# Retention and a gated feed-forward layer in one kernel: weight sums on another engine and at another place, and a cast and a decay factor that change places

## The chip, the cores and the metric

The kernel runs on one core of a Trainium2 chip. A core has five engines with a queue of instructions each: TensorE (PE, with its weight loads shown apart as PEld), VectorE (DVE), ScalarE (ACT), GpSimd (POOL) and SyncE (SP), which here only issues transfers. The engines meet by semaphores alone. The metric is the device time of one execution in microseconds (us); lower is better.

## The reference, cut to what matters

```python
# q, k, v: (8 batches, 8 heads, 576 positions, 64), float32
scores = q @ k^T / sqrt(64)
gamma  = 1 - 2 ** (-5 - head)
ret    = (scores * gamma ** (i - j) for j <= i, else 0) @ v
x      = ret, heads side by side, as (4608 tokens, 512)
out    = (sigmoid(x @ w_gate) * (x @ w_val)) @ w_out      # 512 -> 1536 -> 512
```

The decay gamma ** (i - j) splits into gamma ** i on the row of q and gamma ** (-j) on the row of k. In a sum over j, the second factor may stand on k or on v: the score with j is always multiplied by row j of v, and so is row j of k in the running state k^T v.

## The kernel before, in words

**Retention.** The first 768 columns of x are made by a start-up part that works on pairs of tiles. The rest is cut into 30 steps, s = 0 to 29, each of 128 positions of one batch (STEPS, L101). Step s loads its k, q and v from HBM (`load`, L161), each 256 KB as 128x512 float32, and casts them to bf16 (`cast_qk`, L397; `cast_v`, L410): q is multiplied by a table of gamma ** i (`qtab`), k by a table of gamma ** (-j) (`ktab`), and v is copied. From s = 11 on (SCALED_V, L408), ScalarE casts k plainly and GpSimd multiplies v by `ktab`. A transfer on SP's queue (`cross`, L418) then turns q and k into T_s; for s = 0, 1 and 7 TensorE does that (`turn_step`, L596). The order of one step is written in `casts_to` (L870): issue the loads of a later step, cast k, cast q, turn, cast v. TensorE makes scores, the products k^T v and the values out of this (`slot`, L709, for one step; `slot_of_two`, L725, for two). Copies to x and to the running state follow piece by piece (`after`, L828). `next_slot` (L881) calls the slot of step s and then the casts of step s+3.

**Feed-forward.** x is worked off in blocks of columns (BLOCKS, L344): 512 columns made by the start-up part, then the two small blocks of 256 at columns 512 and 768, called the first and the second 256 block here, then seven of 512. In the small ones `h_units` (L899) makes gate and value for two rows of 128 at a time, fc = 0, 2, 4, 6, 8, 10: the gate product goes to a bank of PSUM and ScalarE takes its sigmoid (L911), the value product goes to the next bank and VectorE multiplies both (L913). These banks come from a ring of three, so the value product of fc + 2 takes the bank that the sigmoid of fc has read. `op_units` (L1246) multiplies by w_out.

The blocks of 512 use a multiplication scheme with seven products of quarter matrices in place of eight (`quarter_units`, L988; `quarters`, L1101). It needs sums of quarters of the weights: sums into tables of their own (`w_sums`, L336, and `wo_sums`, L310, i = 0, 1, 3) and one in place per group (i = 2), which overwrites a quarter of w_gate, w_val or w_out. An in-place sum may come only after the small blocks, which need the raw weights, have read that quarter.

**Order.** All of it is written out by hand. A loop (L1535 to L1580) goes through the blocks; for each unit i of TensorE's work it adds one entry of `weight_sums` at odd i in the two small blocks (L1554), the in-place sums that PLACES (L1085) puts there, and one piece of the retention's work. Each engine does its instructions in the order in which they were written.

Of the kernel before, what the change touches and what calls it, by code (L numbers as in the profile page):

```python
# [16 lines left out]
def kernel(  # L17
# [19 lines left out]
    nc = tc.nc  # L37
# [272 lines left out]
    def wo_sums(i, part, parts, eng=nc.vector):  # L310

        fp = slice(part * (NFC // 2) // parts, (part + 1) * (NFC // 2) // parts)
        b11, b12, b21, b22 = (wo_sb[:, r::2, c:c + DM // 2][:, fp] for r in range(2) for c in (0, DM // 2))
        t1, t2, t4 = (wt_sb[:, j, fp] for j in range(3))
        to, a, b = ((t1, b12, b11), (t2, b22, t1), (b12, b22, b12), (t4, b21, t2))[i]
        eng.tensor_tensor(out=to, in0=a, in1=b, op=ALU.subtract)
# [19 lines left out]
    def w_sums(kind, i, u, eng):  # L336

        a11, a12, a21, a22 = w_quarters(kind, u)
        s1, s2, s4 = (wt3_sb[kind][j][:, u] for j in range(3))
        to, a, b, op = ((s1, a21, a22, ALU.add), (s2, s1, a11, ALU.subtract), (a21, a11, a21, ALU.subtract),  # L340
                        (s4, a12, s2, ALU.subtract))[i]
        eng.tensor_tensor(out=to, in0=a, in1=b, op=op)
# [50 lines left out]
    def by_halves(x):  # L393

        return x.rearrange("p (y m) d -> p y m d", y=2)

    def cast_qk(s, i, eng):  # L397
        c = STEPS[s][1]
        if i == 1:
            natural_qk[s] = nat_pool.tile([P, 2, M, P], BF16, tag="qk", name=f"qk_{s}")  # L400
        to = natural_qk[s][:, i].rearrange("p m (y d) -> p y m d", y=2)
        if i == 1 and s >= SCALED_V:
            nc.scalar.copy(out=to, in_=by_halves(loaded[s][0]))
            return
        tab = (qtab, ktab)[i][:, c, :].rearrange("p (y m) -> p y m", y=2).unsqueeze(3).to_broadcast([P, 2, M, D])
        eng.tensor_tensor(out=to, in0=by_halves(loaded[s][1 - i]), in1=tab, op=ALU.mult)  # L406

    SCALED_V = 11  # L408

    def cast_v(s, eng):  # L410
        natural["v", s] = nat_pool.tile([P, H, D], BF16, tag="v", name=f"v_{s}", bufs=6)
        if s >= SCALED_V:
            tab = ktab[:, STEPS[s][1], :].unsqueeze(2).to_broadcast([P, H, D])
            nc.gpsimd.tensor_tensor(out=natural["v", s], in0=loaded[s][2], in1=tab, op=ALU.mult)  # L414
        else:
            eng(out=natural["v", s], in_=loaded[s][2])
# [453 lines left out]
    def casts_to(s):  # L870
        while done["cast"] <= min(NS - 1, s):
            x = done["cast"]
            loads_to(x + (AHEAD[x] if x < len(AHEAD) else 2))
            cast_qk(x, 1, nc.gpsimd)
            cast_qk(x, 0, nc.vector if x < 2 else nc.gpsimd)
            if x not in TURNED:
                cross(x)
            cast_v(x, on_dve if x == 0 else on_pool)
            done["cast"] += 1
# [108 lines left out]
    def quarter_units(gvs, t0):  # L988
# [82 lines left out]
        def value(fc):  # L1071
# [3 lines left out]
            for kc in range(NKC):  # L1075
# [6 lines left out]
        return quarter, value  # L1082

    EARLY = ((10, "g01"), (13, "g05"), (13, "g02"))
    PLACES = (((1, 0), "w", 0), ((1, 3), "g", 1), ((2, 0), "g", 0), ((2, 6), "o", 2), ((2, 7), "o", 0),  # L1085
              ((2, 10), "g", 2), ((2, 17), "w", 1), ((2, 43), "o", 1))
    TURN_AT = -1
    CASTS_AT = (2, 12)
    SECOND = 7
# [431 lines left out]
    casts_to(1)  # L1521

    weight_sums = [lambda kind=kind, u=u, i=i: w_sums(kind, i, u, nc.vector) for kind, u in (("w", 1), ("g", 2)) for i in (0, 1, 3)]
    weight_sums += [lambda u=u, i=i: wo_sums(i, u, 3) for u in range(3) for i in (0, 1, 3)]

    SPARE = {}
    for at, kind, u in PLACES:
        SPARE.setdefault(at, []).append((lambda u=u: wo_sums(2, u, 3)) if kind == "o" else (lambda kind=kind, u=u: w_sums(kind, 2, u, nc.vector)))
# [83 lines left out]
```

## Time and profile before

| | us |
|---|---|
| median of the runs | 309.91 |
| lowest, highest run | 309.65, 313.43 |
| the profiled execution | 310.84 |
| its span, first to last instruction | 308.9 |

| engine | busy us in the span | share |
|---|---|---|
| PE | 301.0 | 97% |
| DVE | 235.7 | 76% |
| ACT | 199.3 | 65% |
| POOL | 193.0 | 62% |

The profiled execution lies 0.93 us above the median. Its span leaves 1.94 us before the first and after the last instruction. The profile's page gives these sums; an answer of its timeline gives each instruction with its start, its duration and, in brackets, how long its engine stood idle before it and who ended that. Where a date is given below ("at 61.07") it is microseconds from the start of the span. The first 256 block starts at 51.12, the second at 70.32, the first block of 512 at 89.50. TensorE's granted clock is 1.00 in all stages.

### The profile page before, as it was taken

How to read it: one execution, taken by the hardware profiler on the slowest of the kernel's cores; microseconds unless marked ns; L12 is line 12 of the kernel's file. 1: busy time of each engine (PE TensorE's matmuls, PEld its weight loads, DVE VectorE, ACT ScalarE, POOL GpSimd, SP SyncE). 2: the span in 40 equal slices, each digit the busy share in tenths (PEclk: the TensorE clock that was granted, in tenths of full speed). 3: DMA queues.
4: the chain of work that ended last, by engine and by line, in shares of the span. 5: the costliest groups of instructions: out<-in, count | busy, mean ns of one | idle time of the engine just before them, and what ended most of it. 6: DMA issues, size and time to landing. Idle time of an engine off the chain costs nothing.

```text
span 308.9 us, 10407 instructions
## 1 busy us (share of the span) xinstructions
PE 301.0 (97%) x4286; PEld 235.8 (76%) x4286; DVE 235.7 (76%) x469; ACT 199.3 (65%) x408; POOL 193.0 (62%) x221
## 2 busy tenths in 40 slices
PE   8999999999999999999899999999999999999995
PEld 7674456868768778877788788878887888788874
DVE  6957957977889797698669976986699659844963
ACT  6755454535469648964797389737973797359720
POOL 5785653644576897579557965796578607810780
PEclk9999999999999999999999999999999999999999
DMA  7999999989999997990779589946881182004013
GB/s 222 341 371 387 347 272 211 219 168 151 246 191 221 270 218 171 227 219 2 141 175 254 120 139 203 252 95 138 191 211 47 36 280 96 4 2 137 3 34 102
DMA packets 145423, 54.97 MB, mean 178 GB/s; under 512 B 124384, under 2 KB 137696, under 8 KB 145376
## 3 DMA queue, kind: packets, MB, share of 16 engines
q1 hardware_dynamic: 144352, 53.66, 71.1%
q8 instruction: 33, 0.54, 0.7%
q10 hardware_dynamic: 1024, 0.66, 0.7%
q14 instruction: 14, 0.11, 0.1%
HBM read 37.75 MB, written 9.44 MB: 153 GB/s over the span
## 4 chain that ended last, share of the span: by engine, by line
PE 89%; DVE 4%; ACT 3%; POOL 1%; issue 1%; DVEq 0%
PE gatea L1027 11%; PE qa L1134 10%; PE qe L1134 9%; PE wa L1027 8%; PE h L1076 7%; PE gatee L1027 6%; PE we L1027 4%; PE op L1250 3%; PE op L1475 3%; PE gateg L1027 3%; PE hg L1326 3%; PE hv L1326 3%; PE h_g L908 3%; PE h_v L908 2%; PE val L689 2%; PE wg L1027 2%
## 5 line engine op out<-in xcount | busy, mean ns | idle before, releaser
L1027 PEld LDWEIGHTS <-wg_sb 128*128 128x128 bf16 x336 | 32.9, 98 | 5.6
L1050 POOL TENSOR_TENSOR gv<-gv,wu 128x512 bf16<-128x512 bf16 x14 | 16.3, 1166 | 31.7 <-DVE wu L1062 31.7
L1134 PEld LDWEIGHTS <-gsum 128*128 128x128 bf16 x312 | 29.9, 98 | 3.7
L406 POOL TENSOR_TENSOR qk<-q,qtab 128x512 bf16<-128x512 f32 x28 | 30.7, 1098 | 1.9 <-PE wa L1027 1.3
L963 POOL TENSOR_TENSOR gsum<-gv 128x512 bf16<-128x512 bf16 (+1 forms) x28 | 27.6, 987 | 5.3 <-DVE gv L1050 5.2
L1027 PEld LDWEIGHTS <-wgt_sb 128*128 128x128 bf16 x252 | 24.6, 98 | 3.4
L1076 PE MATMUL h<-xT,wv_sb 128*128 128x512 bf16 x112 | 26.5, 379 | 0.0
L1027 PE MATMUL gatea<-xsum,wg_sb 128*128 128x256 bf16 x168 | 25.2, 273 | 0.0
L1134 PEld LDWEIGHTS <-gv 128*128 128x128 bf16 x228 | 21.8, 98 | 4.0
L1027 PEld LDWEIGHTS <-wv_sb 128*128 128x128 bf16 x224 | 21.9, 98 | 3.6 <-issue 1.1
L406 POOL TENSOR_TENSOR qk<-k,ktab 128x512 bf16<-128x512 f32 x11 | 12.2, 1113 | 19.9 <-DMA k<-in_k_dram 14.9
L675 DVE TENSOR_TENSOR pt<-row,tri 128x512 bf16<-128x512 f32 (+1 forms) x36 | 20.0, 596 | 4.0 <-PE row L666 2.9
L1050 POOL TENSOR_TENSOR gv<-gv,ws 128x512 bf16<-128x512 bf16 x14 | 17.1, 1221 | 7.3 <-DVE ws L1065 7.3
L414 POOL TENSOR_TENSOR v<-v,ktab 128x512 bf16<-128x512 f32 x19 | 21.5, 1130 | 0.1
L1065 DVE TENSOR_TENSOR gs<-gatea,gs 128x512 f32<-128x512 f32 x21 | 14.4, 685 | 9.0 <-PE gatea L1027 8.4
L1062 DVE TENSOR_TENSOR gu<-gatee,gu 128x512 f32<-128x512 f32 x21 | 14.4, 687 | 8.4 <-ACT gateg L1054 3.5
L1079 DVE TENSOR_TENSOR gv<-gv,h 128x512 bf16<-128x512 bf16 x28 | 18.4, 678 | 2.4 <-PE h L1076 2.4
L1048 ACT ACTIVATE gv<-gs 128x512 bf16<-128x512 f32 x21 | 13.6, 647 | 9.6 <-DVE gs L1065 9.6
L1076 PEld LDWEIGHTS <-wv_sb 128*128 128x128 bf16 x112 | 11.0, 98 | 10.4
L1027 PEld LDWEIGHTS <-wvt 128*128 128x128 bf16 x168 | 16.4, 98 | 2.5 <-issue 0.6
L986 POOL TENSOR_TENSOR xsum<-xT 128x512 bf16<-128x512 bf16 x6 | 7.0, 1158 | 18.0 <-ACT xT L762 13.1
L762 ACT CAST xT<-val 128x512 bf16<-128x512 f32 x22 | 12.5, 592 | 8.1 <-PE val L705 8.1
(192 smaller groups left out, 859.5 us busy)
## 6 DMA issues: line engine op xcount, KB each, us to landing
k<-in_k_dram SPq DMA_DIRECT2D x26, 256.0 KB, 3.9
q<-in_q_dram SPq DMA_DIRECT2D x26, 256.0 KB, 4.3
v<-in_v_dram SPq DMA_DIRECT2D x26, 256.0 KB, 4.6
out_dram<-ob SPq DMA_DIRECT2D x24, 256.0 KB, 3.0
wg<-in_moe_w_gate_dram SPq DMA_DIRECT2D x12, 256.0 KB, 5.4
wv<-in_moe_w_val_dram SPq DMA_DIRECT2D x12, 256.0 KB, 5.1
wo<-in_moe_w_out_dram SPq DMA_DIRECT2D x12, 256.0 KB, 4.9
v32p<-in_v_dram SPq DMA_DIRECT2D x6, 256.0 KB, 4.5
```

What stands on the lines that cost most here:

```text
L406: eng.tensor_tensor(out=to, in0=by_halves(loaded[s][1 - i]), in1=tab, op=ALU.mult)
L414: nc.gpsimd.tensor_tensor(out=natural["v", s], in0=loaded[s][2], in1=tab, op=ALU.mult)
L675: nc.vector.tensor_tensor(out=t[:, y, 0:n].rearrange("p i m t -> p (i m) t"), in0=rows_tile[ss[0]][y][:, 0:n].rearrange("p i m t -> p (i m ...
L908: nc.tensor.matmul(ps[:, i], lhsT=w_sb[:, kc, (fc + i) * P:(fc + i + 1) * P], rhs=xT(kc, slice(t0, t0 + n)), start=(kc == 0), stop=(kc == ...
L963: nc.gpsimd.tensor_tensor(out=s3, in0=a11, in1=a21, op=ALU.subtract)
L1027: nc.tensor.matmul(ps[:, f], lhsT=w[:, kc, f * P:(f + 1) * P], rhs=x[:, kc], start=(first and f == 0 and kc == 0), stop=(f == 1 and kc == ...
L1050: eng.tensor_tensor(out=to, in0=to, in1=src, op=ALU.mult)
L1062: nc.vector.tensor_tensor(out=me["u2"], in0=e, in1=me["u2"], op=ALU.add)
L1076: nc.tensor.matmul(ps, lhsT=wv_sb[:, kc, fc * P:(fc + 1) * P], rhs=xT(kc, slice(t0, t0 + 512)), start=(kc == 0), stop=(kc == NKC - 1))
L1079: nc.vector.tensor_tensor(out=gvs[fc], in0=gvs[fc], in1=ps, op=ALU.mult)
L1134: nc.tensor.matmul(ps[:, b], lhsT=left(fp)[:, b * P:(b + 1) * P], rhs=right(fp), start=(first and fp == 0 and b == 0), stop=(fp == NFC // ...
L1326: nc.tensor.matmul(ps, lhsT=(wg_sb if what == "g" else wv_sb)[:, kc, fc * P:(fc + 1) * P], rhs=xT(kc, slice(0, 4 * P)), start=(kc == 0), s ...
```

## The change

Three things change.

- `wo_sums` for the nine sums of w_out into tables runs on GpSimd; it ran on VectorE. Its places in the order stay.
- The five in-place sums of w_gate and w_val are put at units 4, 6, 8, 10 and 14 of the second 256 block (w = 1, counted from n_h = 12: -8, -6, -4, -2, 2). They stood at units 12 and 15 of that block and 0, 10 and 17 of the first block of 512. The in-place sum of w_out's first group moves from unit 7 to unit 17 of that block.
- `SCALED_V = 11` becomes a function: for s = 3 to 9, too, ScalarE casts k, and GpSimd multiplies v by `ktab`. Steps 0, 1, 2 and 10 stay as they were.

```diff
-        if i == 1 and s >= SCALED_V:
+        if i == 1 and scaled_v(s):
             nc.scalar.copy(out=to, in_=by_halves(loaded[s][0]))
             return
...
-    SCALED_V = 11
+    def scaled_v(s):
+
+        return 3 <= s <= 9 or s >= 11
...
-        if s >= SCALED_V:
+        if scaled_v(s):
             tab = ktab[:, STEPS[s][1], :].unsqueeze(2).to_broadcast([P, H, D])
             nc.gpsimd.tensor_tensor(out=natural["v", s], in0=loaded[s][2], in1=tab, op=ALU.mult)
...
-    PLACES = (((1, 0), "w", 0), ((1, 3), "g", 1), ((2, 0), "g", 0), ((2, 6), "o", 2), ((2, 7), "o", 0),
-              ((2, 10), "g", 2), ((2, 17), "w", 1), ((2, 43), "o", 1))
+    PLACES = (((1, -8), "g", 0), ((1, -6), "w", 0), ((1, -4), "g", 1), ((1, -2), "w", 1), ((1, 2), "g", 2), ((2, 6), "o", 2), ((2, 17), "o", 0), ((2, 43), "o", 1))
...
-    weight_sums += [lambda u=u, i=i: wo_sums(i, u, 3) for u in range(3) for i in (0, 1, 3)]
+    weight_sums += [lambda u=u, i=i: wo_sums(i, u, 3, nc.gpsimd)
+                    for u in range(3) for i in (0, 1, 3)]
```

## The prediction

> **What bounds the kernel.** I read the engine sums on the page first, then the waits, then the timelines from 50 to 106 us, where all the edits lie.
>
> ```profile
> PE 301.0 (97%) x4286; PEld 235.8 (76%) x4286; DVE 235.7 (76%) x469; ACT 199.3 (65%) x408; POOL 193.0 (62%) x221
> ```
>
> TensorE is busy for 301.0 of 308.9 us, and the change touches none of its work. So a gain can only come out of its idle time, and whatever makes TensorE wait is added to the end, unless a later idle stretch takes it up. Between 89.5 and 106 the timeline of PE shows three waits:
>
> ```profile
> 97.76 0.60 PE L1027 MATMUL wa<-xsum,wv_sb 128*128 128x256 bf16 x4 [0.17 <-ACT wu L1009]
> ...
> 100.33 0.60 PE L1027 MATMUL wa<-xsum,wvt 128*128 128x256 bf16 x4 [0.23 <-ACT wg L1054]
> ...
> 105.45 0.60 PE L1027 MATMUL wa<-xsum,wv_sb 128*128 128x256 bf16 x4 [0.59 <-DVE ws L1065]
> ```
>
> 0.17 + 0.23 + 0.59 = 0.99 us. This is what lighter VectorE and GpSimd queues could win there. The waits, counted over the whole span, tell what the price could be:
>
> ```profile
> POOL qk L406 <- DMA k<-in_k_dram: 14.9, 9, 4.0
> ACT gv L911 <- PE h_g L908: 10.2, 11, 2.1
> ```
>
> GpSimd's casts of k wait for the load of k, 9 times and up to 4.0 us: they start when k lands. That costs nothing now, since nothing urgent stands behind them on GpSimd. ScalarE's sigmoids in the two 256 blocks wait for TensorE alone: ScalarE is there before the gate product is done. The timelines of POOL, ACT and PE, one after the other, put dates to it:
>
> ```profile
> 73.51 1.05 POOL L406 TENSOR_TENSOR qk<-k,ktab 128x512 bf16<-128x512 f32 x1 [2.65 <-PE val L705]
> ...
> 79.42 1.04 POOL L406 TENSOR_TENSOR qk<-k,ktab 128x512 bf16<-128x512 f32 x1 [1.01 <-DMA k<-in_k_dram]
> ...
> 84.24 1.28 POOL L406 TENSOR_TENSOR qk<-k,ktab 128x512 bf16<-128x512 f32 x1 [2.22 <-DMA k<-in_k_dram]
> ```
> ```profile
> 75.64 0.60 ACT L911 ACTIVATE gv<-h_g 128x512 bf16<-128x512 f32 x1 [1.58 <-PE h_g L908]
> ...
> 80.07 0.60 ACT L911 ACTIVATE gv<-h_g 128x512 bf16<-128x512 f32 x1 [2.09 <-PE h_g L908]
> ```
> ```profile
> 77.19 1.04 PE L908 MATMUL h_v<-xT,wv_sb 128*128 128x256 bf16 x8
> ...
> 81.62 1.04 PE L908 MATMUL h_v<-xT,wv_sb 128*128 128x256 bf16 x8
> ```
>
> The k of steps 6, 7 and 8 land at about 73.5, 79.4 and 84.2. The sigmoids are those of fc = 4 and fc = 8 of the second block; the matmuls are the value products of fc = 6 and fc = 10, which take the banks that those sigmoids free.
>
> **Part 1: k on ScalarE (steps 3 to 9).** Seven casts of 0.62 us (L403, 19 of them at 618 to 642 ns; in a row they start 0.52 apart) come to ScalarE: 7 x 0.52 = 3.6 us of work, and ScalarE stands idle over half of that stretch. The work is hidden; the wait is not. The casts stand in ScalarE's queue where `casts_to` is called, right behind a slot. ScalarE works in order, so everything behind the cast waits for k to land. With the next instruction's old date, and its new one 0.52 after the landing: step 3 lands at 56.06, the sigmoid behind it moves from 54.42 to 56.6; step 4 at 61.07, a sigmoid from 59.49 to 61.6; step 5 at 68.06, the copies that empty val_1 from 63.48 to 68.6; step 6 at 73.51, those of val_2 from 68.46 to 74.0; step 7 at 79.42, those of val_3 from 73.64 to 79.9; step 8 at 84.24, the sigmoid of fc = 8 from 80.07 to 84.75; step 9 at 88.36, the copy of an output from 87.11 to 88.9.
>
> TensorE feels what exceeds its cover. Step 3: the value product of fc = 4 (56.42) needs the first of these sigmoids, done at 57.15; with VectorE's copy of T_1 behind it, 1.1 us late. Step 4 gives 1.2, step 5 (val_2 needs the banks of val_1) 2.1. Step 6: the copy that frees a bank for the gate of fc = 2, 74.8 in place of 72.07 for that product, 2.8. Step 7: two copies of val_3 (0.16 apart), then the sigmoid of fc = 4 at 80.25 to 80.85; the value product of fc = 6 starts at 80.9 in place of 77.19: 3.7. Step 8: sigmoid until 85.35, the value product of fc = 10 at 85.4 in place of 81.62: 3.8. These do not add up. The landings are dates of the loads, not of TensorE: a TensorE that is 3.7 late meets k8 with only 0.1 left to wait. Behind k8 the copies of val_4 follow before the turn of step 7 (82.85); VectorE's share of them, with a product (0.60 apart), a sum (0.20), a state (0.33) and one in-place sum (0.33 to 0.77), ends at 87.2 to 87.6 in place of 83.03. So TensorE leaves the second block 4.2 us late (3.7 to 4.6). Step 9 then has cover: ScalarE comes to it at about 87.9.
>
> The landings stay, I take it. SP issues from 41 to 98 without a gap, each transfer waits in the program for the one eight before it, and the DMA engines are 79 to 110% busy in every stretch from 50 to 106. The turns that now wait for ScalarE are issued late enough: that of step 6 at 78.48 (its k cast done at 74.1), of step 8 at 87.50 (84.9).
>
> **Part 2: GpSimd.** It loses 7 casts of k (1.04), 7 casts of v become products (L416 0.62, L414 1.04), and 9 sums come. No such sum stands on POOL in the trace; the nearest rows with this shape, bf16 and two inputs are L986 at 1.16 and L963 at 1.20. I take 1.17. The sum is -7.3 + 2.9 + 10.5 = +6.1 us, in a stretch (64 to 96) where POOL is busy for 16.5 of 32 us, waiting for loads. In its queue the sums stand ahead of q6, q7, q8 and q9. By my count q8 ends at 87.8 in place of 86.5, so the turn of step 8 goes 0.3 later than 87.50; its scores come at 111.7. Cost 0; without that cover, the 0.3. The sums are done by 91.2, ahead of the in-place sum at 93.45 that needs them.
>
> **Part 3: VectorE.** Nine sums leave (0.41 to 0.68, together 4.2 us). Five in-place sums (2.5 us together) move from 84.2 to 98.8 into the second block, and one of two at 93.45 (2.19 for both) moves behind. So the chain at 95.9 to 105.5 (VectorE's gs, ScalarE's copies, TensorE's wa) gets free of some 2.8 us of VectorE's work from 91.5 on, and GpSimd, whose step 11 casts are tied to loads, is ready in time for the products at 100.8 that set the 0.59. Bounds: nothing, or all of the 0.99. I take 0.9, since each of the three waits is far below the work removed ahead of it.
>
> A two-input sum on VectorE costs 0.42 alone, and up to 0.94 beside a running GpSimd instruction:
>
> ```profile
> 61.04 0.42 DVE L342 TENSOR_TENSOR wgt_sb<-wg_sb 128x512 bf16<-128x512 bf16 x1
> ...
> 62.78 0.85 DVE L342 TENSOR_TENSOR wgt_sb<-wgt_sb,wg_sb 128x512 bf16<-128x512 bf16 x1
> ```
>
> GpSimd's cast at 62.32 runs beside the second. So the five cost 2.1 to 4.7 us in the second block, where 2.8 us of sums and 0.8 us of earlier in-place sums leave.
>
> **The sum.** +4.2 - 0.9 = +3.3 us. From the first 512 block on TensorE is busy but for scattered waits, of which the largest, 0.89 at 148.7, is no wait for data in the profile; I count on none to take the delay up. The profiled execution's 310.84 would become 314.1 (span 312.2); on the median of the runs it is 309.91 + 3.3 = 313.2. Bounds: with landings 1 us earlier and all idle time won, 3.7 - 1.0 - 1.0 = +1.7; with nothing won and a bad second block, +4.6 + 0.4 = +5.0. That is 311.6 to 314.9.
>
> **Rivals.** First, *not slower*: the loads run ahead. The place is the load of k8. If, with GpSimd's queue shorter by k, the turns and so the loads behind them came 4.2 us sooner (k8 before 80.1), ScalarE would find each k landed, and only Part 3 is left: -1.0 to 0, 308.9 to 309.9. Against it: SP's queue shows no turn that waits long for GpSimd in these steps, and the loads are full. Chance 0.12.
>
> Second, *slower by over 2%*: the waits add up, because loads begin to follow TensorE. The place is SP's queue, where the loads stand behind turns that wait for ScalarE. It decides when a k cast ends after its turn's old issue date (4.4 us of room at step 6, 2.6 at step 8). Then each step pays its own delay: 1.1 + 1.2 + 2.1 + 2.8 + 3.7 + 3.8 = 14.7, 324.6. Chance 0.07.
>
> Third, *VectorE becomes the second bound*: its in-place sums and GpSimd's new sums block each other. If each of the five waits out a whole GpSimd sum (1.17), that is 5.9 us more in a stretch where ScalarE's waits have already bunched VectorE's work; 2.5 us more than it idles from 72 to 88 (3.4); 1 us to either side, that is 1.5 to 3.5 on top: 314.7 to 316.7. For it speaks the 0.85 above; against it, that no such row exceeds 0.94. Chance 0.13. The Trainium skill, "SBUF — State Buffer", section "Who interferes with whom", speaks for this rival: a VectorE instruction with two SBUF inputs and a GpSimd instruction that reads SBUF exclude each other, and the one that comes second is blocked for the whole of the first. By that rule the five would cost up to 0.42 + 1.17 = 1.59 each; the trace agrees that they delay each other, and shows 0.94 as the longest of this line.
>
> **Chances and range.** The forecast holds 0.68. A difference of 2% (6.2 us) is about what a measurement of this kernel tells from no change. Over 2% slower (from 316.1) are the second rival and part of the third: 0.12; over 2% faster nothing gives: 0.01; within 2%: 0.87. The range 310.0 to 317.0 takes in the forecast and the third rival, and reaches toward the first.
>
> **What would show it.** In the profile after, ScalarE's casts L403 between 55 and 90 wait for the loads of k, seven times and in all about 20 us or more; the sigmoids L913 behind them come late; TensorE has waits for ScalarE of about 4 us in all between 56 and 88, and the first 512 block starts at 93 to 94 in place of 89.50. The waits of 0.17, 0.23 and 0.59 are gone. GpSimd's nine sums last about 1.17 each. I am wrong if k lands at other dates than 56.1, 61.1, 68.1, 73.5, 79.4, 84.2, 88.4; if TensorE's delay at the start of the first 512 block is not kept to the end; or if VectorE's in-place sums last over 1 us each.

## The result, and the profile after

The changed kernel ran in 315.09 us (median of 5 runs, 314.27 to 315.44); the kernel before, on the same chip, in 310.23. The ratio is 1.0126, with a 95% interval of 1.0078 to 1.0173. A second measurement, told below, gave 1.0120 [1.0091, 1.0150]. On the 309.91 us of the prediction these are +3.9 and +3.7 us; the prediction said +3.3 (a ratio of 1.0106). The profiled execution took 315.12 us, its span 313.0.

The page's sums for the kernel after, with the share of the span in brackets:

```profile
PE 301.0 (96%) x4270; PEld 235.8 (75%) x4286; DVE 233.4 (75%) x460; ACT 202.0 (65%) x415; POOL 197.7 (63%) x223
```

TensorE does the same 301.0 us of work, so the whole loss is idle time of TensorE. ScalarE has 2.7 us more work and GpSimd 4.7. The waits of the kernel after (total, number, longest) name what is new:

```profile
ACT qk L403 <- DMA k<-in_k_dram: 16.1, 7, 3.5
...
DVE gv L915 <- ACT gv L913: 3.5, 3, 1.4
...
DVE xT L811 <- ACT share L803: 3.1, 1, 3.1
...
PE h_v L910 <- ACT gv L913: 1.2, 2, 0.7
...
PE h_g L910 <- ACT ob L942: 1.1, 1, 1.1
```

The waits for k, which were GpSimd's in the profile before, are now ScalarE's. Behind them VectorE waits for ScalarE's sigmoids and copies, and TensorE for both. ScalarE's own timeline of the kernel after shows one such place:

```profile
79.98 0.62 ACT L403 CAST qk<-k 128x512 bf16<-128x512 f32 x1 [2.64 <-DMA k<-in_k_dram]
80.50 0.43 ACT L803 COPY share<-val 128x128 f32<-128x128 f32 x2
80.82 0.61 ACT L913 ACTIVATE gv<-h_g 128x512 bf16<-128x512 f32 x1
...
84.74 0.62 ACT L403 CAST qk<-k 128x512 bf16<-128x512 f32 x1 [1.88 <-DMA k<-in_k_dram]
85.26 0.59 ACT L913 ACTIVATE gv<-h_g 128x512 bf16<-128x512 f32 x1
```

The first sigmoid is that of fc = 4. It stands behind two copies, which stand behind a cast that waits 2.64 us for its load. None of them needs this k. TensorE's timeline of the kernel after, with all its waits over 0.15 us for another engine from 60 to 92 us and the first product of the first 512 block:

```profile
63.09 1.03 PE L910 MATMUL h_v<-xT,wv_sb 128*128 128x256 bf16 x8 [0.48 <-ACT gv L913]
...
75.46 1.03 PE L910 MATMUL h_g<-xT,wg_sb 128*128 128x256 bf16 x8 [1.14 <-ACT ob L942]
...
81.48 1.03 PE L910 MATMUL h_v<-xT,wv_sb 128*128 128x256 bf16 x8 [0.74 <-ACT gv L913]
...
87.35 0.38 PE L604 MATMUL turn<-ident,qk 128*128 128x128 bf16 x4 [0.42 <-ACT xT L797]
...
88.39 0.38 PE L604 MATMUL turn<-ident,qk 128*128 128x128 bf16 x4 [0.65 <-DVE xT L813]
...
94.81 0.60 PE L1029 MATMUL gatea<-xT,wg_sb 128*128 128x256 bf16 x4
```

Four waits are for ScalarE, 2.78 us together. The first 512 block starts at 94.81 in place of 89.50. But 1.24 us of that arises before these blocks: the first 256 block itself starts at 52.36, not 51.12, though the start-up is the same code. So the right measure is a stage, from the start of the first 256 block to that of the first 512 block: 42.45 us in place of 38.38, +4.07. From there to the end of the span it takes 218.2 us in place of 219.4.

Nine sums on GpSimd, in the groups of instructions of the kernel after from 50 to 106 us (total, mean ns of one, idle time before):

```profile
L316 POOL TENSOR_TENSOR wt_sb<-wo_sb,wt_sb 128x512 bf16<-128x512 bf16 x6 | 7.1, 1182 | 0.2
...
L316 POOL TENSOR_TENSOR wt_sb<-wo_sb 128x512 bf16<-128x512 bf16 x3 | 3.8, 1275 | 0.0
```

10.9 us in all, 1.21 each, where 1.17 was expected. VectorE's five in-place sums of the same stretch, in its timeline:

```profile
79.16 0.57 DVE L342 TENSOR_TENSOR wg_sb<-wg_sb 128x512 bf16<-128x512 bf16 x1
...
82.30 1.02 DVE L342 TENSOR_TENSOR wv_sb<-wv_sb 128x512 bf16<-128x512 bf16 x1
...
84.50 1.34 DVE L342 TENSOR_TENSOR wg_sb<-wg_sb 128x512 bf16<-128x512 bf16 x1
...
87.22 0.92 DVE L342 TENSOR_TENSOR wv_sb<-wv_sb 128x512 bf16<-128x512 bf16 x1
...
92.40 1.26 DVE L342 TENSOR_TENSOR wg_sb<-wg_sb 128x512 bf16<-128x512 bf16 x1
```

They last 5.1 us together, where the prediction had 2.1 to 4.7. The one at 87.22 stands ahead of the copy xT (L813, 88.06) for which TensorE waits 0.65 us at 88.39.

### The profile page after: what moved, and what is told of

Same layout as the page of the kernel before. It is cut to its first block, busy times and chain, and to the rows that moved or that the text cites. A ratio compares the mean times of both kernels' runs of the same rounds, so it can differ in the third digit from the quotient of the medians.

```text
span 313.0 us, 10392 instructions
## 1 busy us (share of the span) xinstructions
PE 301.0 (96%) x4270; PEld 235.8 (75%) x4286; DVE 233.4 (75%) x460; ACT 202.0 (65%) x415; POOL 197.7 (63%) x223
## 4 chain that ended last, share of the span: by engine, by line
PE 76%; DMA 7%; SPq 6%; DVE 5%; ACT 2%; issue 2%; POOL 2%; DVEq 0%; ACTq 0%
PE gatea L1029 11%; PE qa L1135 10%; PE qe L1135 9%; PE wa L1029 8%; PE h L1078 7%; PE gatee L1029 6%; PE we L1029 4%; PE hv L1327 3%; PE op L1476 3%; SPq L182 3%; PE gateg L1029 3%; DMA k<-in_k_dram 2%; PE hg L1327 2%; PE wg L1029 2%; DMA wv<-in_moe_w_val_dram 2%
## 5 line engine op out<-in xcount | busy, mean ns | idle before, releaser
L416 POOL TENSOR_TENSOR v<-v,ktab 128x512 bf16<-128x512 f32 x26 | 29.3, 1128 | 1.3 <-DMA v<-in_v_dram 1.2
L403 ACT CAST qk<-k 128x512 bf16<-128x512 f32 x26 | 15.5, 625 | 16.1 <-DMA k<-in_k_dram 16.1
L1078 PE MATMUL h<-xT,wv_sb 128*128 128x512 bf16 x105 | 24.9, 379 | 0.4
L1078 PEld LDWEIGHTS <-wv_sb 128*128 128x128 bf16 x112 | 11.0, 98 | 10.2
```

Of the source, the lines that this page charges most:

```text
L1078: nc.tensor.matmul(ps, lhsT=wv_sb[:, kc, fc * P:(fc + 1) * P], rhs=xT(kc, slice(t0, t0 + 512)), start=(kc == 0), stop=(kc == NKC - 1))
```

## The experiments

The theory to be tested: ScalarE's queue, stopped by the loads of k, makes TensorE late; the work of the casts costs nothing; and the stops don't add up, since each ends at the date of a load. The rivals: the work itself; stops that add up; and the two other parts of the change (VectorE and GpSimd blocking each other).

Two tables first, since all runs are read against each other. Ratios are over the kernel before on the same chip, and the us are the ratio times 309.91.

| kernel | ratio [95% interval] | us |
|---|---|---|
| the change | 1.0126 [1.0078, 1.0173] | +3.9 |
| the change again | 1.0120 [1.0091, 1.0150] | +3.7 |
| k on ScalarE alone | 1.0082 [1.0046, 1.0118] | +2.5 |
| sums and places alone | 1.0053 [1.0014, 1.0093] | +1.6 |
| a wait without the work | 1.0102 [1.0066, 1.0139] | +3.2 |
| the work without a wait | 0.9985 [0.9961, 1.0009] | -0.5 |
| k of step 8 alone | 1.0107 [1.0069, 1.0145] | +3.3 |
| k and sums | 1.0081 [1.0049, 1.0113] | +2.5 |
| k and places | 1.0089 [1.0059, 1.0118] | +2.8 |
| the change, k cast later | 1.0031 [1.0008, 1.0055] | +1.0 |
| k cast later alone | 1.0017 [0.9998, 1.0037] | +0.5 |
| k cast later, and places | 1.0022 [0.9998, 1.0047] | +0.7 |
| k cast later, and sums | 1.0023 [1.0003, 1.0042] | +0.7 |

The second table is read from one profiled execution of each: the start of the first 256 block, the time from it to the first 512 block over the 38.38 us of before, when ScalarE starts to cast the k of step 8, or to glance at it (k8; in the kernel before, in sums and places alone and in the work without a wait GpSimd casts it), how long after that the first 512 block starts, and the time from there to the end of the span.

| kernel | first 256 block | stage over before | k8 | k8 to first 512 block | rest |
|---|---|---|---|---|---|
| before | 51.12 | 0 | 84.24 | 5.26 | 219.4 |
| the change | 52.36 | +4.07 | 84.74 | 10.07 | 218.2 |
| the change again | 50.92 | +1.99 | 81.89 | 9.40 | 218.5 |
| k on ScalarE alone | 51.34 | +2.87 | 83.09 | 9.50 | 218.3 |
| a wait without the work | 51.55 | +1.84 | 82.17 | 9.60 | 218.2 |
| k of step 8 alone | 51.62 | +4.33 | 83.25 | 11.08 | 217.6 |
| k and sums | 51.46 | +1.23 | 81.81 | 9.26 | 217.6 |
| k and places | 51.50 | +4.77 | 84.49 | 10.16 | 217.9 |
| sums and places alone | 52.43 | +0.89 | 88.91 | 2.79 | 219.7 |
| the work without a wait | 51.04 | -0.40 | 82.68 | 6.34 | 217.9 |
| the change, k cast later | 51.44 | +0.10 | 84.15 | 5.77 | 218.8 |
| k cast later alone | 51.08 | -0.39 | 83.32 | 5.75 | 218.6 |
| k cast later, and places | 52.27 | +2.28 | 86.85 | 6.08 | 218.8 |
| k cast later, and sums | 51.39 | +0.26 | 84.79 | 5.24 | 220.6 |

The two executions of the change differ by 2 us in the stage, so the first table decides what a kernel costs, and the second only where. (The profiled execution of "k cast later, and places" was its longest, 313.78 us against a median of 310.39; its stage says little of the kernel. Those of "sums and places alone", "k and places" and "k cast later, and sums" were the longest of theirs too, those of "the change again" and "k and sums" the shortest.)

### k on ScalarE alone

```diff
 # the change, with
-    PLACES = (((1, -8), "g", 0), ((1, -6), "w", 0), ((1, -4), "g", 1), ((1, -2), "w", 1), ((1, 2), "g", 2), ((2, 6), "o", 2), ((2, 17), "o", 0), ((2, 43), "o", 1))
+    PLACES = (((1, 0), "w", 0), ((1, 3), "g", 1), ((2, 0), "g", 0), ((2, 6), "o", 2), ((2, 7), "o", 0),
+              ((2, 10), "g", 2), ((2, 17), "w", 1), ((2, 43), "o", 1))
...
-    weight_sums += [lambda u=u, i=i: wo_sums(i, u, 3, nc.gpsimd)
-                    for u in range(3) for i in (0, 1, 3)]
+    weight_sums += [lambda u=u, i=i: wo_sums(i, u, 3) for u in range(3) for i in (0, 1, 3)]
```

> Only the first part: ScalarE casts k and GpSimd multiplies v in steps 3 to 9; the sums of w_out stay on VectorE and the in-place sums at their old places. Theory of the waiting queue: this part carries the whole loss, +4.2 us (3.7 to 4.6) by the prediction, ratio 1.012 to 1.015; ScalarE's casts of k wait about 16 us in seven waits, and the first 512 block starts about 4 us late counted from the start of the first 256 block. The waits of 0.17, 0.23 and 0.59 in the first 512 block stay, so nothing is won back. Rival of VectorE's port: the loss comes from the sums on GpSimd beside VectorE's in-place sums, so this kernel loses clearly less than the change did (under 1.006).

Measured: 1.0082, +2.5 us. TensorE's waits of this kernel between 56 and 106 us, those over 0.15 us that name another engine:

```profile
62.04 1.03 PE L910 MATMUL h_v<-xT,wv_sb 128*128 128x256 bf16 x8 [0.86 <-ACT gv L913]
...
69.90 0.31 PE L691 MATMUL val<-pt,v 64*64 64x64 bf16 x14 [0.67 <-DVE xT L813]
...
79.77 1.03 PE L910 MATMUL h_v<-xT,wv_sb 128*128 128x256 bf16 x8 [0.52 <-ACT gv L913]
...
85.94 0.61 PE L604 MATMUL turn<-ident,qk 128*128 128x128 bf16 x8 [0.57 <-ACT xT L797]
...
95.00 0.60 PE L1029 MATMUL gatea<-xsum,wgt_sb 128*128 128x256 bf16 x4 [0.46 <-DVE xsum L988]
```

That is most of the loss, less than the +4.2 expected, and over the 1.006 that the rival allowed, though the interval reaches below it. Two things follow. Its k8 is cast at 83.09, 31.75 us after the start of the first 256 block, and not 33.12 as in the profile of before: the stop ends 1.4 us sooner, and the stage is 1.3 us less late than the +4.2. And the waits of 0.17, 0.23 and 0.59 in the first 512 block are gone, though VectorE's work is where it was; another, of 0.46 at 95.00, has come. Both expectations of "stay" (the landings, and these waits) failed.

### A wait without the work, and the work without a wait

```diff
 # the kernel before, at the place where the change casts k, steps 3 to 9
+            if 3 <= x <= 9:
+                nc.scalar.copy(out=peek, in_=loaded[x][0][:, 0, 0:1])
```
```diff
 # the kernel before, at the same place
+            if 3 <= x <= 9:
+                for _ in range(4):
+                    nc.scalar.copy(out=spare, in_=ktab[:, 0, 0:1].to_broadcast([P, 96]))
```

> The kernel before, and in steps 3 to 9 ScalarE copies one column of the loaded k (128x1) into a tile that nobody reads, at the place where the change casts k. GpSimd goes on casting k. So ScalarE gets the wait for the load and almost none of the work. Theory of the waiting queue: most of the loss is there, +2.5 to +4 us (ratio 1.008 to 1.013), with 14 to 17 us of waits of that copy. Rival, that the work of the casts on ScalarE is the cost: under +1 us (ratio below 1.003).

> The kernel before, and in steps 3 to 9 four copies of 128x96 out of a table into a tile that nobody reads, on ScalarE at the place where the change casts k: work of about the cast's length, without a load to wait for. Theory of the waiting queue: under +0.5 us (ratio below 1.002). Rival, that the work is the cost: +1 us or more.

Measured: 1.0102 with the wait, 0.9985 with the work. ScalarE's timeline of the first and of the second, at one of the seven places each:

```profile
82.17 0.19 ACT L876 COPY peek<-k 128x1 f32<-128x1 f32 x1 [2.72 <-DMA k<-in_k_dram]
```
```profile
77.58 1.17 ACT L877 CAST spare<-ktab 128x96 bf16<-128x96 f32 x4
```

Seven copies of 0.19 us that wait for k (15 us in six waits; 14 to 17 were expected) cost 3.2 us of time; seven times 1.17 us of work, each about twice the cast's 0.62, that wait for no load cost nothing that can be measured. The loss is the stop of the queue. This is the clearest pair of the study: GpSimd's work, VectorE's sums and the in-place sums are in both as before.

### k of step 8 alone

```diff
 # the kernel before, with
-        return s >= 11
+        return s == 8 or s >= 11
```

> The kernel before, with ScalarE's cast of k and GpSimd's product of v for step 8 alone, out of the steps 3 to 9 (sums and places as before). The prediction said that the delays of the single steps do not add, since each is the date of a load: then step 8 alone, the last with a wait, gives nearly all that the seven give (+2.5 us in k_alone): +1.8 to +2.8 us, ratio 1.006 to 1.009. Rival: the delays add, and one step of seven gives about a seventh to a third of it: +0.4 to +0.9, ratio 1.001 to 1.003.

Measured: 1.0107, +3.3 us, against +2.5 for all seven and the +1.8 to +2.8 expected. ScalarE's and TensorE's timelines of this kernel:

```profile
83.25 0.62 ACT L403 CAST qk<-k 128x512 bf16<-128x512 f32 x1 [5.14 <-DMA k<-in_k_dram]
83.78 0.59 ACT L913 ACTIVATE gv<-h_g 128x512 bf16<-128x512 f32 x1
```
```profile
84.42 1.03 PE L910 MATMUL h_v<-xT,wv_sb 128*128 128x256 bf16 x8 [2.67 <-ACT gv L913]
86.08 1.01 PE L604 MATMUL turn<-ident,qk 128*128 128x128 bf16 x8 [0.63 <-ACT xT L797]
```

In the change ScalarE waits 1.88 us for k8, with this cast alone 5.14: the six earlier stops only use up what the last would cost anyway. The delays do not add. A single cast of 0.62 us at a place where its data is five us away makes the whole loss.

### The cast one step later

```diff
 # the change, steps 3 to 9: allocate qk in the old place, cast k and turn one call of casts_to later
+            while late:
+                k_cast(late[0])
+                if late[0] not in TURNED:
+                    cross(late[0])
+                late.pop(0)
...
-            cast_qk(x, 1, nc.gpsimd)
+            if 3 <= x <= 9:
+                natural_qk[x] = nat_pool.tile([P, 2, M, P], BF16, tag="qk", name=f"qk_{x}")
+            else:
+                cast_qk(x, 1, nc.gpsimd)
...
-            if x not in TURNED:
+            if 3 <= x <= 9:
+                late.append(x)
+            elif x not in TURNED:
                 cross(x)
```

> The changed kernel, but the cast of k on ScalarE, and the turn behind it, stand one call of casts_to later for steps 3 to 9, so that k has landed when ScalarE comes to it; the loads keep their order. All other parts of the change stay. Theory of the waiting queue: the waits of the casts shrink to under 3 us together, TensorE loses at most 1 us before the first 512 block, and with what that block wins the ratio is 0.996 to 1.003. Rivals: if the work on ScalarE or VectorE's port is the cost, the ratio stays at 1.008 or more. What may go wrong by the first theory too: the turn comes some 6 us later, and scores that need it could wait for it.

Measured: 1.0031, +1.0 us, at the upper end of what was expected (1.003); 2.9 us of the change's 3.9 are gone with the stop. ScalarE's timeline of this kernel at k7 and k8 has no wait at either cast:

```profile
78.67 0.61 ACT L875 CAST qk<-k 128x512 bf16<-128x512 f32 x1
...
84.15 0.62 ACT L875 CAST qk<-k 128x512 bf16<-128x512 f32 x1
```

Its stage is 0.10 us longer than that of the kernel before. It uses the same engines, the same work and the same loads as the change; only the cast and the turn behind it come later.

### Sums and places alone

```diff
 # the change, with
-        return 3 <= s <= 9 or s >= 11
+        return s >= 11
```

> Only the other two parts: nine sums of w_out on GpSimd and the in-place sums in the second 256 block; k stays on GpSimd in steps 3 to 9. Theory of the waiting queue: a gain of 0.5 to 1.2 us (ratio 0.996 to 0.998), since the three waits of 0.17, 0.23 and 0.59 at the start of the first 512 block go and nothing makes TensorE wait before it. Rival of VectorE's port: in-place sums of 1 us or more beside GpSimd's sums make VectorE late in the second 256 block, 0.5 to 2 us slower (ratio 1.002 to 1.006).

Measured: 1.0053 [1.0014, 1.0093]. The gain that the prediction's third part expected is not there; it is a loss. TensorE's two largest waits for another engine behind the start-up:

```profile
80.54 0.32 PE L660 MATMUL row<-T 64*64 64x64 bf16 x16 [0.78 <-DMA T<-qk]
...
108.47 0.60 PE L1029 MATMUL wa<-xsum,wv_sb 128*128 128x256 bf16 x4 [1.42 <-DVE ws L1067]
```

The first is for a turn that was issued no later than in the kernel before (74.84, 22.4 us after the start of the first 256 block in both), so it is not shown to be the sums' doing. The second is: the 0.59 has not gone, it has become 1.42. The sum of VectorE there stands behind GpSimd's products of gv, and these start 12.1 us after the first 512 block (103.77 - 91.70) in place of 11.3 (100.76 - 89.50): 0.8 us later, and 1.42 - 0.59 is 0.83. GpSimd isn't out of room at that place, since it sits idle for 1.66 us just before, ahead of its cast of q for step 11 at 101.63. SP's timeline leads further back:

```profile
86.65 1.70 SPq L167 DMA_DIRECT2D v<-in_v_dram  x1
91.16 1.23 SPq L422 DMA_TRANSPOSE T<-qk  x1
...
98.91 1.31 SPq L170 DMA_DIRECT2D v<-in_v_dram  x2
```

SP issues nothing from 88.35 to 91.16. Next in its queue is the turn of step 8, whose q GpSimd casts from 89.91 to 91.13, with sums ahead of it in its queue. In the kernel before the same turn went at 87.50, 36.4 us after the start of the first 256 block; here it is 38.7. Behind it stand the loads of step 11: v is issued 7.2 us after the start of the first 512 block (98.91 - 91.70) in place of 6.2 (95.70 - 89.50), and the products that follow are late with it. So with the casts of k still on GpSimd, its nine sums make a turn late, and the turn makes the loads behind it late. This chain is read from one execution of each kernel. GpSimd's timeline shows its own queue stopped by a load, as ScalarE's is in the change:

```profile
79.73 0.61 POOL L418 CAST v<-v 128x512 bf16<-128x512 f32 x1 [2.62 <-DMA v<-in_v_dram]
80.30 1.16 POOL L316 TENSOR_TENSOR wt_sb<-wo_sb,wt_sb 128x512 bf16<-128x512 bf16 x1
81.41 1.15 POOL L316 TENSOR_TENSOR wt_sb<-wo_sb 128x512 bf16<-128x512 bf16 x1
82.52 1.23 POOL L406 TENSOR_TENSOR qk<-k,ktab 128x512 bf16<-128x512 f32 x1
```

The sums, which needed no load, stood 2.62 us behind a wait for v, and the cast of k7 then came behind them. The rival of VectorE's port named the right sign and size, but not this mechanism: of the five in-place sums only one lasted over 1 us here (1.14).

### Which of the two others: k and sums, k and places, the change again

The second kernel is the change with the old PLACES, the third the change with `wo_sums(i, u, 3)` on VectorE.

> The change without its new places: k on ScalarE and the nine sums on GpSimd, the in-place sums where they were. The change lost 1.3 us more than k_alone, where the prediction had it gain 0.9. If the sums on GpSimd are what loses (they block VectorE's two-input sums, and fill GpSimd's queue ahead of the products of the first 512 block), this kernel stays at +3.5 to +4.5 us (ratio 1.011 to 1.014), and its VectorE instructions with two inputs from 74 to 100 us last longer than in k_alone. If the new places lose it, this kernel is at +2 to +2.7 (1.006 to 1.009).

> The change with the nine sums of w_out left on VectorE: k on ScalarE and the in-place sums at the new places. If the sums on GpSimd are the second loss, this kernel is at +1.5 to +2.7 us (1.005 to 1.009), like k_alone or better, since the first 512 block has less VectorE work. If the new places are the second loss (VectorE then has nine sums and five more in-place sums in the second 256 block), it is at +3.5 us or more (1.011 and up).

> The changed kernel itself, beside the kernel before on this chip. It stood at 1.0126 [1.0078, 1.0173], while k_alone, k_and_sums and k_and_places stand at 1.008 to 1.009, each within 0.4%. If sums and places together cost something on top of the moved k, the ratio stays at 1.011 to 1.014 (+3.5 to +4.3 us). If the 1.0126 was high by chance, it comes out at 1.008 to 1.010 (+2.5 to +3.1 us), which is the prediction's +3.3 less its error in the win-back or less.

Measured: 1.0081, 1.0089 and 1.0120. By its expectation the first kernel puts the second loss on the places, and the second puts it on the sums: each answer points to the part that is left out. Either one on top of k costs nothing over k alone (1.0082) that can be measured; both together stand 1.2 us over it. (The picture hangs on how the runs are summed up: the ratios of the medians are 1.0076 for k alone, 1.0108 and 1.0100 for the two, and 1.0157 and 1.0125 for the change, so that by them either part may cost something by itself.) Of the first kernel's expectation that VectorE's instructions would last longer, the sums of x do, 4.04 us against 3.32 with k alone, and the in-place sums don't, 3.2 against 3.6. With half-widths of 0.0030 and 0.0036 the difference of 0.0038 has an interval of about 0.0047 to either side (the root of the sum of their squares): -0.3 to +2.6 us. So it is likely, but not shown, that the two cost something when they come together.

### Which of the two others, without the stop

> The kernel before, with k on ScalarE and v times decay on GpSimd in steps 3 to 9, ScalarE's cast and the turn one call of casts_to later as in cast_later; sums and places stay as before. If the wait for k is the only cost of the first part, the ratio is 0.997 to 1.002, as GpSimd is also 4 us lighter. If the sums on GpSimd were what was left in cast_later (1.0031), this kernel is faster than that one by 0.5 us or more.

> The same with the new places of the in-place sums, the nine sums on VectorE. By the prediction's third part: 0.5 to 0.9 us under late_alone, since VectorE is lighter in the first 512 block. Rival: VectorE is then heavier in the second 256 block by 2.5 us, and nothing is gained, or up to 1 us lost.

> The same with the nine sums on GpSimd, the in-place sums at their old places. If the sums block VectorE (its two-input sums of x, L988, took 4.14 us together in cast_later and 3.33 before), or fill GpSimd's queue, this kernel is 0.5 to 1 us over late_alone. If they only relieve VectorE, it is at late_alone or 0.5 us under it.

(All three cast k one step later; the edits are those above.) Measured: 1.0017, 1.0022, 1.0023, and 1.0031 with both. The differences among them are within the measurement. But a gain of 0.9 us (0.0029) by sums and places together is out: the last stands 0.0014 over the first, and with half-widths of 0.0024 and 0.0020 the interval of that difference is 0.0031 to either side. The waits of the casts are not all gone in these three: ScalarE still waits up to 0.98, 1.56 and 2.13 us for a k, at no cost that can be measured. VectorE's four sums of x (L1003 here) tell what GpSimd's work does to them. First those of "k cast later alone", where VectorE has the nine sums, then those of "k cast later, and sums", and TensorE's wait behind the latter:

```profile
87.86 0.75 DVE L1003 TENSOR_TENSOR xsum<-xT 128x512 bf16<-128x512 bf16 x2
88.53 1.60 DVE L1003 TENSOR_TENSOR xsum<-xT,xsum 128x512 bf16<-128x512 bf16 x2
```
```profile
89.45 1.71 DVE L1003 TENSOR_TENSOR xsum<-xT 128x512 bf16<-128x512 bf16 x2
91.09 2.55 DVE L1003 TENSOR_TENSOR xsum<-xT,xsum 128x512 bf16<-128x512 bf16 x2
```
```profile
92.51 0.60 PE L1044 MATMUL gatea<-xsum,wgt_sb 128*128 128x256 bf16 x4 [0.56 <-DVE xsum L1003]
```

2.35 us against 4.26, and TensorE waits for the last of them. This pair is far apart among the kernels of the study. In the eight with the nine sums on VectorE the four took 2.1 to 3.8 us (3.33 in the kernel before, 3.0 in the mean), in the six with them on GpSimd 2.9 to 4.3 (2.88 in the change, 3.8 in the mean). So VectorE may pay for being spared nine sums with some 0.8 us here, but the ranges overlap, and the sums are long in the kernel before too, where GpSimd has none of the nine. No kernel of the study is faster than the kernel before by more than the measurement can tell.

## Why the prediction was right, and where it was not

**The total and its cause.** +3.3 was predicted, +3.7 to +3.9 measured. The mechanism of Part 1 holds: ScalarE's queue stops (six waits at k3 to k8, 15.7 us together in its timeline; seven and about 20 were predicted, but k9 had landed when ScalarE came to it), the sigmoids and copies behind it come late, TensorE waits; the work is hidden (the work without a wait, -0.5); the delays do not add (step 8 alone, +3.3).

**Part 1 was too large as a term.** 4.2 us (3.7 to 4.6) stands against +2.5 for k alone. The step that failed is "the landings stay": they stay in order, but not in date. Counted from the start of the first 256 block, k8 is cast at 33.12 in the profile of before, and at 32.4, 31.0, 31.8, 30.6, 31.6, 30.4 and 33.0 in the seven executions with the cast (or the glance at k) in the place of the change. The stages of these seven are 1.2 to 4.8 us late, 3.0 in the mean. From k8 on the chain that was worked out is right: 9.46 us from the landing of k8 to the first 512 block were predicted (93.7 - 84.24), 9.3 to 10.2 measured in the six of them with all seven steps. So the delay was the right function of a date, and the date was read from one execution. Whether that one was late by chance, or the change itself brings k8 sooner, the record leaves open. In the seven executions without a cast in that place, SP issues the load of k8 at 27.9 to 30.4 us after the start of the first 256 block (29.24 in the kernel before, 27.90 in the work without a wait, 29.0 in the mean), in the seven with it at 26.7 to 29.6 (27.9 in the mean): the means are 1.1 us apart, and the ranges overlap. Every one of these loads then lands 3.1 to 3.9 us after its issue, so what moves is the date of the issue in SP's queue, not the transfer.

**Part 3 won nothing of its own.** The 0.9 was to come from VectorE's lighter load in the first 512 block. The three waits of 0.17, 0.23 and 0.59 are indeed gone after the change, but also with k alone, with the wait alone and with step 8 alone, where VectorE's work in that block is unchanged (a single other wait of 0.2 to 0.5 stands there in some of these kernels). A TensorE that comes late finds the others ahead: the waits take up a part of the delay. So the sentence "I count on none to take the delay up" looks wrong, and the 0.9 seems to stand under the wrong heading. This is not fully shown: in the work without a wait, which is not late and has VectorE's work as before, only one wait of 0.48 is left there, and its rest of 217.9 is as short as that of the late kernels, so part of the 0.99 belonged to the one execution it was read from. Without the delay, sums and places gain nothing (1.0017 to 1.0031) or lose (1.0053).

**The sum once more.** With the win-back moved to Part 1, Part 1 was predicted at 4.2 - 0.9 = 3.3 and measured at 2.5, 0.8 less; sums and places then add some 1.2 (an interval that takes in zero) where nothing was left to add: 3.3 - 0.8 + 1.2 = 3.7. The errors stand against each other. That the sum came out better than its terms is luck.

**Part 2.** GpSimd's sums lasted 1.21 (1.17 predicted) and cost nothing measurable where k has left GpSimd (k and sums 1.0081, k alone 1.0082). The turn of step 8 goes at 87.88 in the change, close to the 0.3 after 87.50 that was worked out. With the casts of k still on GpSimd, that turn is 2.3 us later in its stage (38.7 against 36.4), and the sums cost 1.6 us together with the new places.

**The rivals.** *Loads run ahead*: k8 came up to 2.8 us sooner, but GpSimd's shorter queue is not needed for it: it came sooner as well with GpSimd's work untouched (the wait without the work, 30.6). *Waits add up*: fell with step 8 alone; and no k came later for TensorE's delay. *VectorE as second bound*: the blocking is there. In-place sums of over 1 us each were named as a sign that the prediction is wrong, and three of five were: 1.02, 1.34 and 1.26. The prediction took 0.94 as the longest that such a sum had lasted, from the rows of L342 alone. The profile of before has longer ones of the same shape on another line, VectorE's sums of x (shortest, median and longest in ns):

```profile
L986 DVE TENSOR_TENSOR xsum<-xT,xsum x14: 424/1149/1258, 89.9 to 276.9; 128x512 bf16<-128x512 bf16 x14
```

Half of them last over 1.1 us, with no sum of w_out on GpSimd; the first, at 89.88, runs beside its product of q at 89.64. In the same way two in-place sums last 1.19 and 1.12 us with k alone, and one 1.20 in the work without a wait. So 0.94 was no ceiling, and the long ones are no mark of the nine sums. The Trainium skill ("SBUF — State Buffer", section "Who interferes with whom") has a VectorE instruction with two SBUF inputs and a GpSimd instruction that reads SBUF exclude each other: the one that comes second is blocked for the whole of the first. By an estimate from that rule one sum would take up to 0.42 + 1.17 = 1.59 us; the longest in this case is 1.34, so the rule is not contradicted. In the change this reached TensorE, before the first 512 block, only with the 0.65 us at 88.39. With +1.2 us (-0.3 to +2.6) for sums and places on top of k, the price of 1.5 to 3.5 us was probably too high.

**What stays open.** Why the profiled execution of the change starts its first 256 block 1.24 us late, and sums and places alone 1.31: starts of 50.9 (the change again) to 52.4 occur with the same start-up code, and no run here separates chance from cause. Why k8 comes sooner on average where ScalarE casts it in the place of the change. And whether the last 1.2 us are real.

## What to carry to other kernels

Before an instruction moves to another engine, look at what it waits for and not only at what it costs: a wait that was harmless in one queue stops everything behind it in the other, and one such stop can cost as much as seven. Put the instruction where its data has most likely landed (here one step later, 2.9 of 3.9 us back), and keep work that needs no load ahead of work that does. A date read from one execution is one draw: where a cost hangs on the date of a load, read several. And a short wait downstream is no sure gain for another edit: a delay upstream may use it up by itself, and the next execution may not have it.

## What was not expected of the hardware

- The load of k8 lands 3.1 to 3.9 us after its issue in all 14 profiled executions, but its issue ranges from 26.7 to 30.4 us after the start of the first 256 block, though SP has the loads in one order in all of them. These are 13 different kernels, so the spread need not be chance.
- A sum of two 128x512 bf16 tiles in SBUF takes 0.41 us on VectorE alone and 1.15 on GpSimd alone, 2.8 times as long. Beside each other they took up to 1.34 on either engine (VectorE's at 84.50 in the change, beside GpSimd's sums from 82.99 to 85.56).
- A copy of a single column (128x1) costs ScalarE 0.19 us; four copies of 128x96 take 1.17.
